# Third product of a block row moved into the next row, partial sums taken up in another order

## The chip, the cores and the metric

The kernel runs on one NeuronCore of a Trainium2 chip. The metric is device time of one execution in microseconds (us). A core has five engines that run side by side, each with its own instruction queue in program order: TensorE (PE, matmuls; PEld is its weight load), VectorE (DVE), ScalarE (ACT), GpSimd (POOL) and SyncE (SP, which here only issues DMAs). They wait for each other through semaphores. TensorE writes its results to PSUM, eight banks, and the other engines bring them to SBUF.

## The reference

Attention with two softmaxes that factor, then a two-layer network over all tokens:

```python
q_s = exp(q - max_d q) / sum_d        # over the head dimension
k_s = exp(k - max_s k) / sum_s        # over the sequence
kv  = einsum('bhsd,bhse->bhde', k_s, v)
x   = einsum('bhsd,bhde->bhse', q_s, kv)   # as 4608 tokens x 512
h   = x @ w_in                             # 512 x 2048
out = maximum(0.01 * h, h) @ w_out         # 2048 x 512
```

q, k and v are 8 batches x 8 heads x 576 x 64, in float32.

## The kernel before, in words

The 4608 tokens are nine tiles of 512. Attention of later batches runs between the matmuls of earlier tiles. For tiles 1 to 6 a plain scheme holds: layer 1 (`layer1`, L561) gives sixteen blocks of 128 hidden features, `leaky` (L571) on ScalarE makes the activations `g`, and layer 2 (`layer2_at`, L938) takes sixteen bf16 matmuls for each 128 tokens (a "tsub"), each ended by a ScalarE copy and a store.

Tiles 7 (called A, `TA`) and 8 (B8, `TB`) are done together, by a scheme that computes a 2x2 block product with seven block products instead of eight, at the cost of sums. Two stages matter.

The first is layer 1 of both tiles: eight block rows, `pair_layer1(i)` (L1027). The token sums s1 to s4 are made once by VectorE (`token_sums`, L831), the weight sums t1 to t4 of each row by GpSimd, two rows ahead (`in_weight_sums`, L811), with `b22`, a float32r copy of a weight block that has two buffers. The products of a row, each two matmuls of 128x512 (bf16 for the first two, float32r for the others), are: the first product `pair_first(i)` into bank px, issued a row ahead and copied out as e1 by ScalarE; t2·s2 added into px, copied out as u2 by VectorE; the second product into bank pw, to which e1 is added; t3·s3 into px, copied out as u3 by VectorE; t1·s1 into bank py, to which u3 is added; t4·a22 into px; and the third product b22·s4, added into py, to which u2 is added. A product that adds into a bank must wait until the copy out of that bank is done. ScalarE's `leaky` turns the sums into activations.

Between the products stand "fills" (`between(n)`, L1067): single layer 2 matmuls of tile 6, whose tsubs 1 to 3 were kept back for that (48 fills; tsub 0 is done ahead of row 0). The order on every engine is the order in which this Python code issues instructions; no planner changes it. The adds of u2 and their `leaky` are put off into the next row by the list `held`.

The second stage is layer 2 of both tiles, L1191 to L1222, again seven products for each tile: first, second, sixth, fifth, seventh, fourth, third (each sixteen matmuls of 128x256). First to second are bf16, the others float32r on row sums r1, r2, r3, r4 made by VectorE (`sums`, `row_sums`), and c22, a copy by ScalarE. r1 and r3 of tile 7 are made ahead in four blocks (`sums_ahead`), three by GpSimd, the last by VectorE. After first, sixth and seventh ScalarE takes a snapshot of the accumulating bank (`snap`: e1, u2, u3), and the next product into that bank must wait for it. `c11`, `c12` and `c22` are VectorE adds that finish quarters of the output. `put` (L1121) issues their DMAs; for tile 8 every other one is issued from ScalarE's queue:

```python
A = dict(t=TA, ..., issue=(nc.sync, nc.sync))
B8 = dict(t=TB, ..., issue=(nc.sync, nc.scalar))
```

Of the kernel before, what the change touches and what calls it, by code (L numbers as in the profile page):

```python
# [26 lines left out]
def kernel(  # L27
# [9 lines left out]
    nc = tc.nc  # L37
# [533 lines left out]
    def leaky(o, ph):  # L571
        nc.scalar.activation(out=o, in_=ph, func=AF.Prelu, alpha=LEAKY_SLOPE)  # L572
# [365 lines left out]
    def layer2_at(t, g, tsub, pool=psO_pool, tag="pout"):  # L938
        po = pool.tile([P, O], FP32, name="pout", tag=tag)
        for j in range(NF):  # L940
            layer2(po, g, tsub, j)
            if j == NF - 1:
                store(t * TT + tsub * P, po, nc.scalar.copy)
            if j % 4 == 3:
                run(t, 16 + 4 * tsub + j // 4)
            yield

    for t in range(1, TA):
        g_sb = []
        for j in range(NF):  # L950
            ph = psB_pool.tile([P, TT], FP32, name="ph", tag=BANK_TAG)
            layer1(j, ph, t * TT, TT)
            if j % 2 == 0:
                g_sb.append(g_pool.tile([P, 2, TT], BF16, name="gj"))
            leaky(g_sb[j // 2][:, j % 2], ph)
            run(t, j)
        for tsub in range(NTS if t < TA - 1 else 1):
            for _ in layer2_at(t, g_sb, tsub, *((psB_pool, BANK_TAG) if t == TA - 1 else ())):
                pass


# [4 lines left out]
    def g7_rows(i):  # L966
        if i == 0:
            g7_pairs.extend(g_pool.tile([P, 2, TT], BF16, name="gj") for _ in range(2))
        for fh in range(2):
            if i < 2:  # L970
                g7[fh * NH + i] = g7_pairs[fh][:, i]
            elif i < 6:
                g7[fh * NH + i] = spent(4 * (4 + fh) + i - 2)
            else:
                g7[fh * NH + i] = spent(4 * 6 + 2 * fh + i - 6)
# [19 lines left out]
    def late_rows(name, n, pool):  # L995
        late[name] = pool.tile([P, NH, M2], F32R, name=n)

    def sums_ahead(n):
        if n == 0:
            for name in ("r3", "r1"):  # L1000
                late_rows(name, name, late["ahead"])
        (ms, h0), (_, h1) = g7_blocks(0)[n], g7_blocks(1)[n]
        for name, x, y, op in (("r1", h1(0), h1(1), ALU.add), ("r3", h0(0), h1(0), ALU.subtract)):
            eng = nc.vector if n == 3 else nc.gpsimd
            eng.tensor_tensor(out=late[name][:, ms], in0=x, in1=y, op=op)

    def bank():
        return psB_pool.tile([P, TT], FP32, name="pp", tag=BANK_TAG)

    def product(ps, w, a, first=True):  # L1010
        for c in range(2):
            nc.tensor.matmul(ps, lhsT=w(c), rhs=a(c), start=(first and c == 0), stop=(c == 1), skip_group_check=True)  # L1012

    def add(o, ps, e):
        nc.vector.tensor_tensor(out=o, in0=ps, in1=e, op=ALU.add)  # L1015

    of = lambda n: (lambda c: late[n][:, c])
    keep = lambda n: late["pool"].tile([P, TT], FP32, name=n)
    firsts, held = {}, []

    def pair_first(i):
        ps, e1 = bank(), keep("e1")
        product(ps, lambda c: w_in_sb[:, c, i * P : (i + 1) * P], lambda c: xT[:, c, XA])
        nc.scalar.copy(out=e1, in_=ps)
        firsts[i] = ps, e1

    def pair_layer1(i, fills):  # L1027
        px, e1 = firsts[i]
        u2, u3 = keep("u2"), keep("u3")
        g7_rows(i)  # L1030
        product(px, of(("t2", i)), of("s2"), False)
        for fn in held:
            fn()
        nc.vector.tensor_copy(out=u2, in_=px)  # L1034
        pw = bank()
        product(pw, lambda c: w_in_sb[:, 2 + c, i * P : (i + 1) * P], lambda c: xT[:, 2 + c, XA])
        if i + 1 < NH:
            pair_first(i + 1)
        add(e1, pw, e1)
        leaky(g7[i], e1)  # L1040
        between(fills[0])
        product(px, of(("t3", i)), of("s3"), False)
        nc.vector.tensor_copy(out=u3, in_=px)
        py = bank()
        product(py, of(("t1", i)), of("s1"))
        between(fills[1])
        add(u3, py, u3)
        leaky(g8(NH + i), u3)
        if i == 0:
            nc.gpsimd.tensor_copy(out=gate, in_=u3[:, 0:1])  # L1050
        product(px, of(("t4", i)), of("a22"), False)
        leaky(g8(i), px)
        between(fills[2])
        product(py, of(("b22", i)), of("s4"), False)
        held[:] = [lambda: add(u2, py, u2), lambda: leaky(g7[NH + i], u2)]
        if i + 2 < NH:
            in_weight_sums(i + 2)
        if i in (2, 4, 6):
            sums_ahead(i // 2 - 1)
# [7 lines left out]
    def between(n):  # L1067
        for _ in range(n):
            next(fill)

    pair_first(0)
    between(2)
    for i in range(NH):
        pair_layer1(i, (2, 2, 2) if i else (1, 2, 1))
    for fn in held:
        fn()
    next(fill, None)
    sums_ahead(3)
    pairs.close()
    last_pool = ctx.enter_context(tc.tile_pool(name="late3", bufs=1, reuse_waits="tile"))  # L1080

# [6 lines left out]
    def product2(ps, a, w, each=False, turns=False, first=True):  # L1088
        order = [(i, m) for i in range(2) for m in range(NH)]
        if turns:  # L1090
            order = [(i, m) for m in range(NH) for i in range(2)]
        for i, m in order:
            nc.tensor.matmul(  # L1093
                ps[i],
                lhsT=a(m)[:, i * P : (i + 1) * P],
                rhs=w(m),
                start=(first and m == 0 and (each or i == 0)),
                stop=(m == NH - 1 and (each or i == 1)),
                skip_group_check=True,
            )  # L1100

    def row_sums(wide, name, n, pool, op, x, y, eng=nc.vector):
        late_rows(name, n, pool)
        for (ms, h0), (_, h1) in zip(wide(0), wide(1)):
            view = lambda s: late[s][:, ms].bitcast(FP32) if isinstance(s, str) else (h0, h1)[s[0]](s[1])
            o = late[name][:, ms]
            if op is None:
                nc.scalar.copy(out=o, in_=view(x))
            else:
                eng.tensor_tensor(out=o, in0=view(x), in1=view(y), op=op)  # L1110
# [3 lines left out]
    plain_w = lambda fh: (lambda m: w_out_sb[:, fh * NH + m, E1])  # L1114
    gu = lambda: g_pool.tile([P, 2, H2], FP32, name="gu", tag="gj")
    out_pairs = lambda: [osb_pool.tile([P, O], FP32, name="out_sb") for _ in range(2)]
    last_pairs = lambda n: [last_pool.tile([P, O], FP32, name=f"{n}{i}") for i in range(2)]
    A = dict(t=TA, g=lambda n: g7[n], wide=g7_wide, each=False, issue=(nc.sync, nc.sync))
    B8 = dict(t=TB, g=g8, wide=g8_wide, each=True, issue=(nc.sync, nc.scalar))

    def put(z, o, half, i, cols):  # L1121
        for n, issue in enumerate(z["issue"]):
# [11 lines left out]
    def first(z):  # L1134
        if z["each"]:
            z["x"] = banks2(True)
        else:
            z["xx"] = psB_pool.tile([P, 2, H2], FP32, name="pq", tag=BANK_TAG)
            z["x"] = [z["xx"][:, i] for i in range(2)]
        product2(z["x"], plain_g(z["g"], 0), plain_w(0), z["each"], turns=True)  # L1140
        snap(z, "e1")

    def second(z):
        z["w"] = banks2(False, psO_pool, "pout")
        product2(z["w"], plain_g(z["g"], 1), plain_w(1), turns=True)

    def sixth(z):
        product2(z["x"], rows("r2"), rows("v2"), z["each"], first=False)
        snap(z, "u2")

    def fifth(z):
        z["y"] = banks2(z["each"])
        product2(z["y"], rows("r1"), rows("v1"), z["each"])

    def seventh(z):
        product2(z["x"], rows("r3"), rows("v3"), z["each"], first=False)
# [11 lines left out]
    def c11(z):  # L1168
        for i in range(2):
            add(z["o1"][i][:, E1], z["w"][i], z["e1"][:, i])  # L1170
            put(z, z["o1"][i], 0, i, E1)
# [9 lines left out]

    def sums(z, n):
        pool = late["ahead"] if n == "r3" else last_pool
        row_sums(z["wide"], n, n, pool, *dict(
            r2=(ALU.subtract, "r1", (0, 0)),
            r3=(ALU.subtract, (0, 0), (1, 0)),
            r4=(ALU.subtract, (0, 1), "r2"),
            c22=(None, (1, 1), None),
        )[n])

    A["o1"], B8["o1"] = out_pairs(), last_pairs("o1")  # L1191
    first(A)
    sums(A, "r2")
    first(B8)
    sums(A, "r4")
    sums(A, "c22")
    second(A)
    c11(A)
    second(B8)
    sixth(A)  # L1200
    fifth(A)
    late["r1"] = strip("r1").rearrange("p a b -> p (a b)")[:, 0 : NH * M2].rearrange("p (m t) -> p m t", t=M2)
    for (ms, _), (_, h1) in zip(g8_wide(0), g8_wide(1)):
        nc.vector.tensor_tensor(out=late["r1"][:, ms], in0=h1(0), in1=h1(1), op=ALU.add)  # L1204
    c11(B8)
    sums(B8, "r2")
    seventh(A)
    A["o2"], B8["o2"] = out_pairs(), last_pairs("o2")
    sixth(B8)
    c22(A)  # L1210
    fourth(A)
# [42 lines left out]
```

## Time and profile before

| | |
|---|---|
| median of 3 runs | 282.3 us (282.01 to 282.64) |
| the profiled execution's own time | 282.73 us |
| its span, first to last instruction | 280.9 us |
| mean granted TensorE clock | 0.997 |
| TensorE busy | 273.1 us (97%) |
| VectorE busy | 216.8 us (77%) |
| ScalarE busy | 170.2 us (61%) |
| GpSimd busy | 81.2 us (29%) |

A line of the timeline has the start (us from the span's start), the duration, the engine, the source line, the operation, the tiles (out<-in) and shapes, and how many like it were merged (x4); in brackets how long the engine was idle just before, and what released it. Lines of a window view have the window, its length, each engine's busy time in it (with the number of instructions) in the order PE, PEld, DVE, ACT, POOL, then the granted TensorE clock, the DMA engines' busy share and GB/s. Ends of matmuls are modelled, so the distance from start to start is the firmer figure.

### The profile page before, as it was taken

What the parts mean: (1) busy time and instruction counts of PE and PEld (TensorE: products, weight loads), DVE (VectorE), ACT (ScalarE), POOL (GpSimd) and SP (SyncE); (2) the same over time, 40 slices, a digit from 0 to 9 for tenths busy, and PEclk for the clock granted to TensorE, in tenths of its full rate; (3) what the DMA queues carried; (4) which work ended last, traced back from release to release, by engine and by line L of the source; (5) the groups of instructions that cost most, each with busy time, mean ns of one, the idle gap of its engine ahead of it and who ended that gap; (6) DMA issues with size and microseconds to landing.
All of it is one profiled execution on the core that took longest, in us unless ns stands there. A gap on an engine that the chain in (4) does not pass through costs nothing. (4 is left out here: it accounts for less than half of the span.)

```text
span 280.9 us, 5223 instructions
## 1 busy us (share of the span) xinstructions
PE 273.1 (97%) x2018; PEld 147.7 (53%) x2018; DVE 216.8 (77%) x303; ACT 170.2 (61%) x302; POOL 81.2 (29%) x103
## 2 busy tenths in 40 slices
PE   8899999999999999999999999999999999999994
PEld 3378644444444444444444444454444555569994
DVE  2995995899999939957794698949958767679951
ACT  3976663783498457754675458664664666654241
POOL 2867360159003004000400084002011798800000
PEclk9999999999999999999999999999999999999998
DMA  7999999987996797099309930430701010101254
GB/s 235 331 209 322 240 256 271 394 277 217 258 389 213 102 386 255 2 228 398 116 4 267 384 84 2 84 77 0 160 0 40 0 37 0 40 19 31 65 113 113
DMA packets 40488, 46.48 MB, mean 165 GB/s; under 512 B 18832, under 2 KB 24208, under 8 KB 40464
## 3 DMA queue, kind: packets, MB, share of 16 engines
q1 hardware_dynamic: 36480, 41.43, 49.5%
q0 software_dynamic: 3504, 4.20, 8.6%
q10 hardware_dynamic: 480, 0.52, 0.6%
q8 instruction: 16, 0.26, 0.4%
q14 instruction: 8, 0.07, 0.1%
HBM read 36.70 MB, written 9.44 MB: 164 GB/s over the span
## 5 line engine op out<-in xcount | busy, mean ns | idle before, releaser
L584 PE MATMUL pout<-w_out_sb,gj 128*128 128x512 bf16 x448 | 103.7, 380 | 0.0
L563 PE MATMUL ph<-xT,w_in_sb 128*128 128x512 bf16 (+1 forms) x512 | 98.8, 352 | 0.3 <-DMA w_in_sb<-in_moe_w_in_dram 0.3
L572 ACT ACTIVATE gj<-ph 128x512 bf16<-128x512 f32 x112 | 63.5, 602 | 19.0 <-PE ph L563 18.5
L563 PEld LDWEIGHTS <-w_in_sb 128*128 128x128 bf16 x512 | 49.7, 98 | 47.6 <-DMA w_in_sb<-in_moe_w_in_dram 0.6
L584 PEld LDWEIGHTS <-gj 128*128 128x128 bf16 x448 | 41.8, 98 | 51.8 <-issue 4.6
L218 POOL CAST vb<-v_raw 128x1152 bf16<-128x1152 f32 x13 | 19.8, 1551 | 83.7 <-DMA v_raw<-in_v_dram 66.4
L578 ACT COPY out_sb<-pout 128x512 f32<-128x512 f32 x24 | 14.0, 584 | 34.8 <-PE pout L584 18.0
L321 DVE TENSOR_REDUCE qsum<-qe 128x36 f32<-128x2304 bf16 (+5 forms) x13 | 20.1, 1542 | 6.4 <-ACT qe L312 6.2
L206 ACT ACTIVATE ke<-k_raw 128x2304 bf16<-128x2304 f32 (+2 forms) x13 | 18.0, 1384 | 8.1 <-DVE k_raw L198 7.6
L328 DVE TENSOR_TENSOR qe<-qe,qrec 128x2304 bf16<-128x2304 bf16 (+5 forms) x13 | 21.5, 1656 | 0.4
L245 DVE TENSOR_REDUCE qmax<-q_raw 128x36 f32<-128x2304 f32 (+5 forms) x13 | 20.0, 1540 | 0.5 <-DMA q_raw<-in_q_dram 0.5
L312 ACT ACTIVATE qe<-q_raw 128x2304 bf16<-128x2304 f32 (+5 forms) x13 | 17.2, 1321 | 4.1 <-POOL q_raw L304 3.1
L198 DVE TENSOR_TENSOR k_raw<-k_raw,kall 128x1152 f32<-128x1152 f32 (+2 forms) x10 | 18.1, 1822 | 0.3
L304 POOL TENSOR_TENSOR q_raw<-q_raw,qmax 128x512 f32<-128x512 f32 (+3 forms) x7 | 11.8, 1680 | 21.2 <-DVE qmax L245 20.9
L1015 DVE TENSOR_TENSOR u<-pp,u 128x512 f32<-128x512 f32 x16 | 11.1, 692 | 8.6 <-PE pp L1012 7.8
L1012 PE MATMUL pp<-s,t 128*128 128x512 f32 x48 | 14.9, 419 | 0.8 <-issue 0.3
L572 ACT ACTIVATE xT<-u 128x512 bf16<-128x512 f32 x14 | 8.8, 630 | 10.9 <-DVE u L1015 10.8
L160 DVE TENSOR_TENSOR t<-t 128x256 f32<-128x256 f32 (+2 forms) x22 | 14.3, 652 | 0.7
L500 ACT CAST xT<-po 128x448 bf16<-128x448 f32 (+3 forms) x31 | 13.3, 513 | 1.6 <-PE po L479 1.6
L361 DVE RECIPROCAL krec<-pokv 128x2 f32<-128x2 f32 x8 | 1.3, 165 | 16.7 <-PE pokv L479 16.7
L304 DVE TENSOR_TENSOR q_raw<-q_raw,qmax 128x2304 f32<-128x2304 f32 (+1 forms) x6 | 13.2, 2202 | 0.2
L790 POOL TENSOR_TENSOR t<-w_in_sb 128x256 fp32r<-128x256 bf16 x16 | 11.4, 711 | 3.3 <-PE pp L1012 3.3
(125 smaller groups left out, 326.0 us busy)
## 6 DMA issues: line engine op xcount, KB each, us to landing
out_dram<-out_sb SPq DMA_DIRECT2D x60, 128.0 KB, 3.9
q_raw<-in_q_dram SPq DMA_DIRECT2D x6, 1152.0 KB, 9.1
v_raw<-in_v_dram SPq DMA_DIRECT2D x6, 1152.0 KB, 11.7
k_raw<-in_k_dram SPq DMA_DIRECT2D x5, 1152.0 KB, 6.3
k_raw<-in_k_dram SPq DMA_DIRECT2D x6, 576.0 KB, 6.5
v_raw<-in_v_dram SPq DMA_DIRECT2D x4, 576.0 KB, 8.0
w_in_sb<-in_moe_w_in_dram POOLq DMA_DIRECT2D x7, 256.0 KB, 6.9
w_out_sb<-in_moe_w_out_dram POOLq DMA_DIRECT2D x6, 256.0 KB, 9.4
```

The source lines that it names most:

```text
L198: eng.tensor_tensor(out=ks, in0=ks, in1=st[b]["kall"][:, hs].unsqueeze(2).to_broadcast([P, n, R, D]), op=ALU.subtract,)
L206: nc.scalar.activation(out=st[b]["ke"][:, :, hs].rearrange("p r h d -> p h r d"), in_=st[b]["k"][:, hs], func=AF.Exp,)
L218: eng.tensor_copy(out=o, in_=i)
L245: nc.vector.tensor_reduce(out=o, in_=st[b]["q"][:, hs, rs], axis=AX.X, op=ALU.max)
L304: eng.tensor_tensor(out=qs, in0=qs, in1=st[b]["qmax", rs.start, hs.start].unsqueeze(3).to_broadcast([P, m, n, D]), op=ALU.subtract,)
L312: nc.scalar.activation(out=q_cols(b, rs, hs).rearrange("p r h d -> p h r d"), in_=st[b]["q"][:, hs, rs], func=AF.Exp,)
L321: nc.vector.reduce_sum(out=qsum, in_=q_cols(b, rs, hs), axis=AX.X)
L328: nc.vector.tensor_tensor(out=qes if out is None else out, in0=qes, in1=st[b]["qrec", rs.start, hs.start].unsqueeze(3).to_broadcast([P, n, ...
L563: nc.tensor.matmul(ph, lhsT=w_in_sb[:, cb, j * P : (j + 1) * P], rhs=xT[:, cb, c0 : c0 + n], start=(cb == 0 and first), stop=(cb == NB - 1 ...
L572: nc.scalar.activation(out=o, in_=ph, func=AF.Prelu, alpha=LEAKY_SLOPE)
L584: nc.tensor.matmul(pout, lhsT=g_sb[j // 2][:, j % 2, tsub * P : (tsub + 1) * P], rhs=w_out_sb[:, j, os], start=(j == 0), stop=(j == NF - 1),)
L1012: nc.tensor.matmul(ps, lhsT=w(c), rhs=a(c), start=(first and c == 0), stop=(c == 1), skip_group_check=True)
```

## The change

Five parts.

1. Tile 6's tsub 0 is done after the function that follows it in the text, and row 0's first product is issued after ten of its sixteen fills. Its copy e1 thus stands ahead of the store's copy on ScalarE.
2. In row 0 the second product, with its add and its `leaky`, is issued ahead of t2·s2, and u2 is copied by ScalarE.
3. In the other rows VectorE's copy u2 comes first, then the second product and the third product of the row before, each with its add; the list `held` is gone. The fills are spread anew: (0, 3, 3) in most rows instead of (2, 2, 2).
4. In the second layer VectorE's sums have another order: r1's last block, r2 of tile 7, r1 of tile 8, then `c11(A)`, r3's last block, r2 of tile 8, `c11(B8)`, and r4 of tile 7 after them. r1 and r2 of tile 8 have names and buffers of their own.
5. `c11(B8)` is issued ahead of `sixth(A)` instead of behind `fifth(A)`. Tile 8's first output pair lies in two buffers of the activation pool.

The number of matmuls of each kind is the same.

```diff
-        for tsub in range(NTS if t < TA - 1 else 1):
-            for _ in layer2_at(t, g_sb, tsub, *((psB_pool, BANK_TAG) if t == TA - 1 else ())):
+        for tsub in range(NTS if t < TA - 1 else 0):
+            for _ in layer2_at(t, g_sb, tsub):
                 pass
...
-    def sums_ahead(n):
+    def sums_ahead(n, names=("r1", "r3")):
...
+    def pair_second(i):
+        e1 = firsts[i][1]
+        ps = bank()
+        product(ps, lambda c: w_in_sb[:, 2 + c, i * P : (i + 1) * P], lambda c: xT[:, 2 + c, XA])
+        add(e1, ps, e1)
+        leaky(g7[i], e1)
+
+    def pair_third(i):
+        py, u2 = thirds[i]
+        product(py, of(("b22", i)), of("s4"), False)
+        add(u2, py, u2)
+        leaky(g7[NH + i], u2)
+
     def pair_layer1(i, fills):
-        px, e1 = firsts[i]
+        px = firsts[i][0]
         u2, u3 = keep("u2"), keep("u3")
         g7_rows(i)
+        if i == 0:
+            pair_second(i)
+            between(1)
         product(px, of(("t2", i)), of("s2"), False)
-        for fn in held:
-            fn()
-        nc.vector.tensor_copy(out=u2, in_=px)
-        pw = bank()
-        product(pw, lambda c: w_in_sb[:, 2 + c, i * P : (i + 1) * P], lambda c: xT[:, 2 + c, XA])
+        if i:
+            nc.vector.tensor_copy(out=u2, in_=px)
+            pair_second(i)
+            pair_third(i - 1)
+        else:
+            nc.scalar.copy(out=u2, in_=px)
         if i + 1 < NH:
             pair_first(i + 1)
-        add(e1, pw, e1)
-        leaky(g7[i], e1)
         between(fills[0])
...
         between(fills[2])
-        product(py, of(("b22", i)), of("s4"), False)
-        held[:] = [lambda: add(u2, py, u2), lambda: leaky(g7[NH + i], u2)]
...
-    pair_first(0)
-    between(2)
+    for n, _ in enumerate(layer2_at(TA - 1, g_sb, 0, psB_pool, BANK_TAG)):
+        if n == 9:
+            pair_first(0)
     for i in range(NH):
-        pair_layer1(i, (2, 2, 2) if i else (1, 2, 1))
-    for fn in held:
-        fn()
+        pair_layer1(i, ((2, 3, 2), *[(0, 3, 3)] * 5, (0, 3, 2), (1, 3, 1))[i])
+    pair_third(NH - 1)
     next(fill, None)
-    sums_ahead(3)
...
-    last_pairs = lambda n: [last_pool.tile([P, O], FP32, name=f"{n}{i}") for i in range(2)]
+    last_pairs = lambda: [gu().rearrange("p a b -> p (a b)") for _ in range(2)]
...
+    def r1_last():
+        late["r1b"] = strip("r1b").rearrange("p a b -> p (a b)")[:, 0 : NH * M2].rearrange("p (m t) -> p m t", t=M2)
+        for (ms, _), (_, h1) in zip(g8_wide(0), g8_wide(1)):
+            nc.vector.tensor_tensor(out=late["r1b"][:, ms], in0=h1(0), in1=h1(1), op=ALU.add)
...
-    A["o1"], B8["o1"] = out_pairs(), last_pairs("o1")
+    A["o1"], B8["o1"] = out_pairs(), last_pairs()
     first(A)
+    sums_ahead(3, ("r1",))
     sums(A, "r2")
     first(B8)
-    sums(A, "r4")
+    r1_last()
     sums(A, "c22")
     second(A)
     c11(A)
+    sums_ahead(3, ("r3",))
     second(B8)
+    sums(B8, "r2")
+    c11(B8)
     sixth(A)
+    sums(A, "r4")
     fifth(A)
-    late["r1"] = strip("r1").rearrange("p a b -> p (a b)")[:, 0 : NH * M2].rearrange("p (m t) -> p m t", t=M2)
-    for (ms, _), (_, h1) in zip(g8_wide(0), g8_wide(1)):
-        nc.vector.tensor_tensor(out=late["r1"][:, ms], in0=h1(0), in1=h1(1), op=ALU.add)
-    c11(B8)
-    sums(B8, "r2")
     seventh(A)
```

More of the change, by code (lines that the diff above doesn't have):

```diff
@@ L1002, in sums_ahead @@
         (ms, h0), (_, h1) = g7_blocks(0)[n], g7_blocks(1)[n]
-        for name, x, y, op in (("r1", h1(0), h1(1), ALU.add), ("r3", h0(0), h1(0), ALU.subtract)):
+        ops = dict(r1=(h1(0), h1(1), ALU.add), r3=(h0(0), h1(0), ALU.subtract))
+        for name in names:
+            x, y, op = ops[name]
             eng = nc.vector if n == 3 else nc.gpsimd
@@ L1018 @@
     keep = lambda n: late["pool"].tile([P, TT], FP32, name=n)
-    firsts, held = {}, []
+    firsts, thirds = {}, {}
     def pair_first(i):
@@ L1045, in pair_layer1 @@
         product(py, of(("t1", i)), of("s1"))
+        thirds[i] = py, u2
         between(fills[1])
@@ L1116 @@
     out_pairs = lambda: [osb_pool.tile([P, O], FP32, name="out_sb") for _ in range(2)]
-    last_pairs = lambda n: [last_pool.tile([P, O], FP32, name=f"{n}{i}") for i in range(2)]
-    A = dict(t=TA, g=lambda n: g7[n], wide=g7_wide, each=False, issue=(nc.sync, nc.sync))
-    B8 = dict(t=TB, g=g8, wide=g8_wide, each=True, issue=(nc.sync, nc.scalar))
+    last_pairs = lambda: [gu().rearrange("p a b -> p (a b)") for _ in range(2)]
+    A = dict(t=TA, g=lambda n: g7[n], wide=g7_wide, each=False, issue=(nc.sync, nc.sync), r1="r1", r2="r2")
+    B8 = dict(t=TB, g=g8, wide=g8_wide, each=True, issue=(nc.sync, nc.scalar), r1="r1b", r2="r2b")
     def put(z, o, half, i, cols):
@@ L1147, in sixth @@
     def sixth(z):
-        product2(z["x"], rows("r2"), rows("v2"), z["each"], first=False)
+        product2(z["x"], rows(z["r2"]), rows("v2"), z["each"], first=False)
         snap(z, "u2")
@@ L1152, in fifth @@
         z["y"] = banks2(z["each"])
-        product2(z["y"], rows("r1"), rows("v1"), z["each"])
+        product2(z["y"], rows(z["r1"]), rows("v1"), z["each"])
     def seventh(z):
@@ L1183, in sums @@
         pool = late["ahead"] if n == "r3" else last_pool
-        row_sums(z["wide"], n, n, pool, *dict(
-            r2=(ALU.subtract, "r1", (0, 0)),
+        name = "r2b" if z is B8 and n == "r2" else n
+        row_sums(z["wide"], name, name, pool, *dict(
+            r2=(ALU.subtract, z["r1"], (0, 0)),
             r3=(ALU.subtract, (0, 0), (1, 0)),
-            r4=(ALU.subtract, (0, 1), "r2"),
+            r4=(ALU.subtract, (0, 1), z["r2"]),
             c22=(None, (1, 1), None),
         )[n])
-    A["o1"], B8["o1"] = out_pairs(), last_pairs("o1")
+    def r1_last():
[3 more added lines that the diff above has]
+    A["o1"], B8["o1"] = out_pairs(), last_pairs()
     first(A)
+    sums_ahead(3, ("r1",))
     sums(A, "r2")
     first(B8)
-    sums(A, "r4")
+    r1_last()
     sums(A, "c22")
@@ L1198 @@
     c11(A)
+    sums_ahead(3, ("r3",))
     second(B8)
+    sums(B8, "r2")
+    c11(B8)
     sixth(A)
+    sums(A, "r4")
     fifth(A)
-    late["r1"] = strip("r1").rearrange("p a b -> p (a b)")[:, 0 : NH * M2].rearrange("p (m t) -> p m t", t=M2)
-    for (ms, _), (_, h1) in zip(g8_wide(0), g8_wide(1)):
-        nc.vector.tensor_tensor(out=late["r1"][:, ms], in0=h1(0), in1=h1(1), op=ALU.add)
-    c11(B8)
-    sums(B8, "r2")
     seventh(A)
-    A["o2"], B8["o2"] = out_pairs(), last_pairs("o2")
+    A["o2"], B8["o2"] = out_pairs(), [last_pool.tile([P, O], FP32, name=f"o{i}") for i in range(2)]
     sixth(B8)
```

## The prediction

> **What bounds the kernel now.** I read the page first (which engine fills the span), then busy time by stretch from 207.29 us on (no instruction ahead of it moves), then the timeline, all engines.
>
> ```profile
> span 280.9 us, 5223 instructions
> ...
> PE 273.1 (97%) x2018; PEld 147.7 (53%) x2018; DVE 216.8 (77%) x303; ACT 170.2 (61%) x302; POOL 81.2 (29%) x103
> ```
>
> ```profile
> 207.29:217.60 10.31, 9.68 (x49) 4.43 (x41) 8.90 (x12) 5.68 (x11) 1.75 (x5) 1.00 0.12 27
> 217.60:246.00 28.40, 28.37 (x122) 15.18 (x121) 19.65 (x31) 18.45 (x32) 23.50 (x35) 1.00 0.09 19
> 246.00:250.19 4.19, 4.06 (x18) 1.89 (x17) 2.99 (x5) 2.04 (x4) 0.00 (x0) 1.00 0.01 2
> 250.19:276.90 26.71, 26.61 (x225) 25.49 (x224) 19.78 (x28) 10.62 (x21) 0.00 (x0) 1.00 0.31 71
> ```
>
> TensorE is the bound, at full clock (the 1.00 behind the POOL column). The change moves matmuls and removes none, so only TensorE's waits can be won or lost. Modelled ends hide short waits in "busy", so I price by distances between starts.
>
> First block row 0. The columns are start, duration, engine, line.
>
> ```profile
> 207.29 3.63 PE L584 MATMUL pout<-w_out_sb,gj 128*128 128x512 bf16 x16
> ...
> 210.76 0.59 PE L1012 MATMUL pp<-xT,w_in_sb 128*128 128x512 bf16 x2
> ...
> 211.44 0.59 ACT L1024 COPY e<-pp 128x512 f32<-128x512 f32 x1
> ...
> 212.13 0.70 PE L1012 MATMUL pp<-s,t 128*128 128x512 f32 x2 [0.35 <-issue]
> 212.25 1.22 DVE L790 TENSOR_TENSOR s<-xT,s 128x1024 fp32r<-128x1024 bf16 x1
> ...
> 213.39 0.68 DVE L1034 COPY u<-pp 128x512 f32<-128x512 f32 x1
> ...
> 213.99 0.68 DVE L1015 TENSOR_TENSOR e<-pp,e 128x512 f32<-128x512 f32 x1
> ...
> 214.22 1.17 PE L1012 MATMUL pp<-s,t 128*128 128x512 f32 x4 [0.29 <-DVE u L1034]
> ...
> 214.70 0.63 ACT L572 ACTIVATE gj<-e 128x512 bf16<-128x512 f32 x1 [0.37 <-DVE e L1015]
> ...
> 215.23 0.60 PE L584 MATMUL pout<-w_out_sb,gj 128*128 128x512 bf16 x2
> ```
>
> Two waits: t2·s2 for ScalarE's copy e1 (ends 212.03), and t3·s3 at 214.22 for VectorE's copy u2, which stood behind the token sum s4 (ends 213.47).
>
> A steady row (3), with the first line from row 1:
>
> ```profile
> 217.60 1.04 PE L1012 MATMUL pp<-xT,w_in_sb 128*128 128x512 bf16 x4
> ...
> 226.78 0.69 DVE L1015 TENSOR_TENSOR u<-pp,u 128x512 f32<-128x512 f32 x1 [1.00 <-PE pp L1012]
> 227.06 1.04 PE L1012 MATMUL pp<-xT,w_in_sb 128*128 128x512 bf16 x4
> ...
> 227.39 0.68 DVE L1034 COPY u<-pp 128x512 f32<-128x512 f32 x1
> ...
> 229.03 0.69 DVE L1043 COPY u<-pp 128x512 f32<-128x512 f32 x1 [0.36 <-PE pp L1012]
> 229.31 0.60 PE L584 MATMUL pout<-w_out_sb,gj 128*128 128x512 bf16 x2
> ...
> 229.87 0.70 PE L1012 MATMUL pp<-a,t 128*128 128x512 f32 x2
> ...
> 230.41 0.61 PE L584 MATMUL pout<-w_out_sb,gj 128*128 128x512 bf16 x2
> ...
> 231.79 1.04 PE L1012 MATMUL pp<-xT,w_in_sb 128*128 128x512 bf16 x4
> ```
>
> Each line with x4 here begins with a row's second product: 217.60 in row 1, 227.06 in row 3, and 231.79 a row (4.73) later. A bf16 matmul takes b = 0.217 (207.29 to 210.76 is sixteen). From 227.06 to 229.31 lie six of them and two float32r products (pairs of matmuls): a pair is p = (2.25 − 1.30) / 2 = 0.475. A row is 10b + 5p = 4.545; the missing 0.19 is t4·a22, which should come at 229.31 + 2b = 229.74 but waits for the copy u3 (229.03 + 0.69 = 229.72) until 229.87, and then needs 0.54 instead of p. So VectorE to TensorE takes 0.15, and TensorE to VectorE 0.19 (t3·s3 ends at 229.31 − p = 228.84).
>
> The second layer of tiles 7 and 8:
>
> ```profile
> 250.19 0.61 PE L1093 MATMUL pq<-w_out_sb,gj 128*128 128x256 bf16 x4
> ...
> 251.77 1.29 DVE L1005 TENSOR_TENSOR r<-xT 128x512 fp32r<-128x512 bf16 x2 [0.70 <-ACT xT L572]
> ...
> 252.98 0.69 DVE L1110 TENSOR_TENSOR r<-r,gj 128x512 fp32r<-128x512 f32 x1
> ...
> 255.32 0.69 DVE L1110 TENSOR_TENSOR r<-gj,r 128x512 fp32r<-128x512 bf16 x1
> ...
> 257.11 8.26 PE L1093 MATMUL pq<-v,r 128*128 128x256 f32 x64
> 257.66 0.75 DVE L1015 TENSOR_TENSOR out_sb<-pq,gu 128x256 f32<-128x256 f32 x2
> ...
> 258.32 2.35 DVE L1204 TENSOR_TENSOR r<-xT 128x1024 fp32r<-128x1024 bf16 x2
> 259.30 0.59 ACT L1132 COPY gu<-pq 128x512 f32<-128x512 f32 x1 [2.89 <-PE pq L1093]
> 260.59 0.76 DVE L1015 TENSOR_TENSOR o<-pq,gu 128x256 f32<-128x256 f32 x2
> ...
> 261.05 1.38 ACTq L1124 DMA_DIRECT2D out_dram<-o  x2
> 261.25 2.36 DVE L1110 TENSOR_TENSOR r<-r,xT 128x1024 fp32r<-128x1024 f32 x2
> 263.14 0.59 ACT L1132 COPY gu<-pq 128x512 f32<-128x512 f32 x1 [3.25 <-DMA out_dram<-o]
> ...
> 265.20 2.08 PE L1093 MATMUL pq<-v,c 128*128 128x256 f32 x16
> 267.12 2.08 PE L1093 MATMUL pq<-o,r 128*128 128x256 f32 x16
> ```
>
> A float32r product takes 1.92 (265.20 to 267.12). The four from 257.11 to 265.20 should take 7.75 (the first, after a bf16 one, 1.99: its snapshot starts at 259.30, some 0.2 behind its end) and take 8.09: 0.34 is sixth(B8)'s wait for r2 of tile 8, ready at 263.61.
>
> **The change, part by part.** Call T the start of first(A), 250.19 now.
>
> Row 0. e1's copy moves ahead of the store's copy on ScalarE, and the first product goes after ten of tile 6's fills, so t2·s2 finds all it needs. But u2's copy goes to ScalarE, whose order becomes: leaky of e1, then that copy. The leaky needs VectorE's add of e1, which comes where u2's copy stands now, behind s4: 213.39 to 214.07. Leaky from 214.10 to 214.73 (0.03 and 0.63, as at 214.70), copy until about 215.24, and TensorE 0.1 later (212.03 to 212.13) at 215.34. By then it has done 25 bf16 matmuls and one product from 207.29, in both kernels, so t3·s3 is 1.12 later. From there 1.01 for the two products (214.22 to 215.23), 3b, p, 2b and p bring the start of row 1's second product to 218.39, against 217.60.
>
> Rows 1 to 6. The third product b22·s4 now comes in the next row, behind the second product. From a row's t2·s2 the gap to t3·s3 is 4b + p = 1.34, while u2's copy takes 0.19 + 0.68 + 0.15 = 1.02: hidden. VectorE then has copy u2, add e1, add u2 of the row before, and copy u3 at 0.61 spacing (226.78 to 227.39): 0.19 + 3 × 0.61 = 2.02, about when t3·s3 lets it start (1.34 + p + 0.19 = 2.00). It is ready at 2.02 + 0.69 + 0.15 = 2.86; t4·a22 now has three fills ahead and comes at 1.34 + 2p + 3b = 2.94. Hidden by 0.08; with that cover gone a row gets its 0.19 back. An unstalled pair between fills stands nowhere in the trace: p (t3·s3 follows fills so) or 0.54 bound it; I take p, the same product behind the same kind of fill. Five rows of 4.545 and row 6 with one fill less (4.33): 241.11, then 245.44.
>
> The b22 buffer comes free a product later, so GpSimd's weight sums may wait a little in its queue; it is busy 23.50 of 28.40 there and each sum is wanted two rows on: nothing. SP's DMAs keep their order. Tile 8's o1 takes two activation buffers of tile 6, whose last reader is a fill ahead of T: nothing.
>
> Row 7. No first product stands between, so u3's copy (2.86) is later than t4·a22 could start (2.73): 2.86 + 0.54 + b + p = 4.09. T = 249.53: 0.66 won.
>
> Second layer. VectorE now does r1's last block, r2(A), r1 of tile 8, c11(A), r3's block, r2 of tile 8, c11(B8), and only then r4(A). r2 of tile 8 is early, so the 0.34 goes. But c11(B8)'s adds are late: VectorE's chain starts at T + 1.58 (251.77) and takes 0.60 (half of 251.77 to 252.98) + 2.34 (252.98 to 255.32) + 2.27 (258.32 to 260.59) + 0.66 (257.66 to 258.32) + 0.60 + 2.27 = 8.74, with no wait for TensorE in it: the first add at T + 10.32. The two output DMAs of c11(B8) that ScalarE issues stand, in its order, now ahead of both of tile 7's snapshots. Queued behind them is the snapshot u2, which frees the bank for seventh(A). The issues begin 0.46 behind the add (260.59 to 261.05), last 1.38, then 0.59 of copy and 0.1: T + 12.85. TensorE could start seventh(A) at T + 6.92 + 1.99 + 1.92 = T + 10.83. So 2.02 is lost, and some 0.07 in the first pair behind it.
>
> How far the issues hold the copy is not shown before: 0 to 1.38. I take 1.38, since the two issues themselves follow one another in ScalarE's row. [...]
>
> The sum against the profiled execution's 282.73 (its median stands 0.43 lower): −0.66 (T) − 0.34 + 2.02 + 0.07 = +1.09, so 283.8 there and 283.4 for the median 282.3. The tail behind TensorE's end keeps its shape.
>
> **The rivals.** 0.2% (0.56 us) is about what the measurement tells from no change.
>
> No change: the copy waits for the adds but not for the issues. It could start at T + 10.32 + 0.76 + 0.04, and seventh(A) at T + 11.81: 0.98 lost, −0.66 − 0.34 + 0.98 + 0.07 = +0.05: 282.4. For it: an issue isn't counted as engine work. Against: the order on the queue.
>
> Faster: the issue of a DMA doesn't hold ScalarE at all, wait included, so snapshot u2 runs at T + 9.1 and seventh(A) is on time: −0.66 − 0.34 = −1.0: 281.3. It decides once the copy is done by T + 10.83. For it: no ScalarE copy of the old kernel stands late because of an issue. Against: none could be late, as the next copy (263.14) came 0.7 behind the issues' end and waited for seventh(A).
>
> Slower still: the 0.08 of cover in the rows is gone, or an unstalled pair costs 0.54. Rows 1 to 6 then keep 4.73, six times 0.19 = 1.1: 284.5. For it: VectorE's four steps fit to 0.02. Against: its spacings have held to 0.01.
>
> **How the numbers follow.** Forecast 0.56, no change 0.14, faster 0.16, slower still 0.14. The forecast's own range is 282.9 to 284.0 (the issues at 0.5 each, or a row's wait half back). The 8-in-10 range takes in no change, half of each of the outer cases: 281.4 to 284.4. Slower takes 0.14 and all but 0.05 of the forecast: 0.65; same 0.17; faster 0.18.
>
> **What would show it.** Right: t3·s3 of row 0 near 215.3, behind ScalarE's copy; rows 4.55 apart without a wait at t4·a22; first(A) near 249.5; a gap of 2 us at the start of seventh(A), ended by ScalarE's gu copy, itself behind two issues on its queue; no wait at sixth(B8). Wrong: first(A) later than 250.2, or seventh(A) right behind fifth(A).

## The result and the profile after

The changed kernel takes 285.05 us (median of six runs, 283.50 to 285.34) against 282.25 for the kernel before: the ratio of the means is 1.0087, 95% interval 1.0061 to 1.0113. Slower, as forecast, but by 2.8 us where 1.1 was said, and outside the range of 281.4 to 284.4. The six runs fall into two groups. Four take 285.01 to 285.34 with a mean granted TensorE clock of 0.993 or 0.994; two take 283.50 and 284.03, with 0.999 and 1.000. The profiled execution (285.34) is one of the four.

The page of the changed kernel, and its busy time by stretch. The columns are the window, its length, then PE, PEld, DVE, ACT, POOL with instructions, the granted clock, DMA share, GB/s:

```profile
span 283.5 us, 5218 instructions
...
PE 272.3 (96%) x2018; PEld 148.3 (52%) x2018; DVE 215.4 (76%) x302; ACT 170.1 (60%) x303; POOL 81.4 (29%) x103
...
PEclk9999999999999999999999999999997999999999
```

```profile
200.00:216.00 16.00, 14.03 (x78) 6.47 (x77) 11.06 (x11) 9.80 (x18) 0.74 (x2) 1.00 0.17 37
216.00:219.50 3.50, 3.50 (x10) 1.71 (x9) 1.04 (x2) 1.23 (x2) 2.21 (x5) 0.51 0.00 0
219.50:258.00 38.50, 38.50 (x202) 23.24 (x201) 28.38 (x43) 24.43 (x44) 22.54 (x33) 1.00 0.10 21
258.00:260.40 2.40, 2.40 (x22) 2.40 (x21) 2.40 (x5) 0.00 (x0) 0.00 (x0) 1.00 0.16 36
260.40:263.90 3.50, 1.62 (x15) 1.42 (x13) 3.50 (x6) 0.59 (x1) 0.00 (x0) 1.00 0.49 110
```

PE is "busy" for all of 216.00 to 219.50, but with ten matmuls, and the granted clock there is 0.51: the 7 in the row of digits. The trace's record of the clock puts the half clock from 216.04 to 219.46, 3.4 us. In the last window PE is busy 1.62 of 3.50 at full clock: a wait. What stands ahead of the slow stretch ("issue" in brackets means that the profile shows nothing that released the engine; ACTq is a DMA issue on ScalarE's queue):

```profile
206.90 2.33 PE L584 MATMUL pout<-w_out_sb,gj 128*128 128x512 bf16 x10
...
211.91 0.60 PE L1014 MATMUL pp<-xT,w_in_sb 128*128 128x512 bf16 x2
212.35 0.59 PE L584 MATMUL pout<-w_out_sb,gj 128*128 128x512 bf16 x2
212.99 0.69 DVE L1017 TENSOR_TENSOR e<-pp,e 128x512 f32<-128x512 f32 x1
213.72 0.63 ACT L572 ACTIVATE gj<-e 128x512 bf16<-128x512 f32 x1 [2.13 <-DVE e L1017]
214.25 0.57 ACT L1055 COPY u<-pp 128x512 f32<-128x512 f32 x1
...
214.92 1.16 PE L1014 MATMUL pp<-s,t 128*128 128x512 f32 x4 [1.97 <-issue]
...
215.92 1.39 PE L584 MATMUL pout<-w_out_sb,gj 128*128 128x512 bf16 x3
...
216.75 1.42 PE L1014 MATMUL pp<-a,t 128*128 128x512 f32 x2
...
219.59 0.60 PE L1014 MATMUL pp<-xT,w_in_sb 128*128 128x512 bf16 x2
```

The chain of row 0 is the forecast one (VectorE's add, leaky, ScalarE's copy, t3·s3). TensorE stands idle for 1.97 us, does t3·s3 and t1·s1 at full rate, and then runs at half.

The second layer:

```profile
251.02 0.61 PE L1108 MATMUL pq<-w_out_sb,gj 128*128 128x256 bf16 x4
...
261.36 0.76 DVE L1017 TENSOR_TENSOR gu<-pq,gu 128x256 f32<-128x256 f32 x2
...
261.81 1.40 ACTq L1139 DMA_DIRECT2D out_dram<-gu  x2
...
263.25 0.59 ACT L1147 COPY gu<-pq 128x512 f32<-128x512 f32 x1 [6.00 <-issue]
263.88 2.17 PE L1108 MATMUL pq<-v,r 128*128 128x256 f32 x16 [1.88 <-ACT gu L1147]
...
277.42 2.08 PE L1108 MATMUL pq<-o,r 128*128 128x256 f32 x16
```

The snapshot starts 0.04 behind the end of the two issues (263.21), 1.13 behind the second add (262.12), though sixth(A) was long done; seventh(A) follows it.

Where the time went, measured from tile 6's first fill of that stage (206.90 after, 207.29 before, as the front part came out 0.39 shorter in this execution): first(A) comes after 44.12 instead of 42.90 (+1.22), the last product's start another 26.40 behind it instead of 24.61 (+1.79). Together +3.01, less 0.39: the span is 2.6 longer.

### The profile page after: what moved, and what is told of

Same layout as the page of the kernel before. It is cut to its first block, busy times and chain, and to the rows that moved or that the text cites. A ratio compares the mean times of both kernels' runs of the same rounds, so it can differ in the third digit from the quotient of the medians.

```text
span 283.5 us, 5218 instructions
## 1 busy us (share of the span) xinstructions
PE 272.3 (96%) x2018; PEld 148.3 (52%) x2018; DVE 215.4 (76%) x302; ACT 170.1 (60%) x303; POOL 81.4 (29%) x103
## 4 chain that ended last, share of the span: by engine, by line
PE 90%; DVE 5%; DMA 2%; issue 1%; ACT 0%; ACTq 0%; SPq 0%; DVEq 0%
PE pout L584 35%; PE ph L563 34%; PE pp L1014 10%; PE pq L1108 7%; DMA k_raw<-in_k_dram 2%; PE po L479 2%; DVE t L160 1%; PE pokv L341 1%; DVE r2b L1125 1%; PE pkv L341 1%; DVE r1b L1210 1%; PE pkv L419 0%; DVE k_raw L410 0%; DVE gu L1017 0%; ACTq L1139 0%
## 5 line engine op out<-in xcount | busy, mean ns | idle before, releaser
L1014 PE MATMUL pp<-s,t 128*128 128x512 f32 x48 | 17.0, 463 | 2.0 <-issue 2.0
L1051 DVE COPY u<-pp 128x512 f32<-128x512 f32 x7 | 4.8, 692 | 10.2 <-PE pp L1014 8.9
L160 DVE TENSOR_TENSOR t<-k_raw 128x512 f32<-128x512 f32 (+1 forms) x11 | 11.2, 1016 | 1.3 <-DMA k_raw<-in_k_dram 1.2
```

The costliest lines, as they stand in the source:

```text
L160: nc.vector.tensor_tensor(out=o, in0=i0, in1=i1, op=ALU.max)
```

## The experiments

Two theories of the clock had to be told apart. A: row 0's wait also costs the clock. B: the drop of the clock has another cause. A third, C, is about the other wait: seventh(A) waits for VectorE's sums, not for the snapshot behind the issues. Nothing is left out of any kernel below; they are compared with the kernel before at 281.89 us (first four) and, on another chip, 281.97 (last four).

**Row 0's copy first.**

```diff
+        if not late_leaky:          # in pair_second; True in row 0
             leaky(g7[i], e1)
...
             nc.scalar.copy(out=u2, in_=px)
+            leaky(g7[i], firsts[i][1])
```

> The changed kernel, with one thing moved: in row 0 ScalarE copies u2 ahead of the leaky of e1, so the copy no longer stands behind VectorE's add of e1. Nothing is left out. Theory A: TensorE's wait of 1.97 us at t3 s3 of row 0 goes, and with it the stretch of 3.4 us at half the granted clock that follows it (another 1.7 us); the mean granted clock is 0.999 to 1.000 in every run, and the time is 285.05 - 2.0 - 1.7 = about 281.4 us, the same within 0.5 us in all runs. Rival B: the drop of the granted clock has another cause and stays: 285.05 - 2.0 = about 283.0 us, with 0.993 to 0.994 in most runs. In both the wait of about 2 us at seventh(A) stays.

Twelve runs: six of 281.22 to 281.55 at 0.999 to 1.000, six of 282.63 to 282.90 at 0.993 or 0.994. Neither theory as it was put: row 0's wait is gone and its slow stretch too, but the profiled execution (282.90) has one elsewhere, behind the other wait:

```profile
216.00:219.50 3.50, 3.50 (x17) 1.97 (x16) 3.09 (x5) 2.00 (x5) 3.32 (x6) 1.00 0.00 0
219.50:258.00 38.50, 38.50 (x216) 24.89 (x214) 29.05 (x44) 22.45 (x41) 20.43 (x30) 1.00 0.13 28
258.00:260.40 2.40, 0.52 (x5) 0.40 (x4) 2.40 (x4) 0.58 (x1) 0.00 (x0) 1.00 0.48 109
260.40:263.90 3.50, 3.50 (x20) 3.50 (x20) 0.18 (x2) 0.59 (x1) 0.00 (x0) 0.54 0.00 0
```

Here seventh(A)'s wait of 1.88 us (258.1 to 260.0) is followed by half clock. So the drop follows either wait, and not in every run.

**The snapshot first.**

```diff
-    c11(B8)
     sixth(A)
+    c11(B8)
```

> The changed kernel, with one thing moved: c11(B8) is issued behind sixth(A), so that on ScalarE the snapshot u2 of tile 7 stands ahead of the two output DMAs; VectorE's, TensorE's and SP's orders are the same. Nothing is left out. Theory A (the two DMA issues, waiting for VectorE's late adds, hold the snapshot): seventh(A) starts 1.9 to 2.1 us earlier, directly behind fifth(A): about 283.1 us in runs with a granted clock of 0.993 to 0.994, about 281.6 us in runs with 0.999 to 1.000. Rival C (seventh(A) waits for VectorE's late row sums, not for the snapshot): no change, 285 us. The wait in row 0 and the drop of the clock stay as they are, in about two runs of three.

Twelve runs: eight of 281.03 to 281.51 at 0.997 to 1.000, four of 282.66 to 283.21 at 0.992 or 0.993: a drop in one run of three, where two of three were expected. The three products sixth(A), fifth(A) and seventh(A), and ScalarE's rows, in the profiled execution, one of the eight:

```profile
255.94 5.99 PE L1108 MATMUL pq<-v,r 128*128 128x256 f32 x48
...
258.13 0.59 ACT L1147 COPY gu<-pq 128x512 f32<-128x512 f32 x1 [2.88 <-PE pq L1108]
259.81 1.39 ACTq L1139 DMA_DIRECT2D out_dram<-gu  x2
261.97 0.59 ACT L1147 COPY gu<-pq 128x512 f32<-128x512 f32 x1 [3.25 <-DMA out_dram<-gu]
```

The issues take the same 1.39, now with nothing waiting behind them, and TensorE no longer waits at seventh(A): its 48 matmuls stand in one row of 5.99. VectorE's and TensorE's orders are untouched, so C falls. Row 0's wait of 1.96 is there, without a drop in this execution; from the first fill first(A) takes 42.46 here and 44.12 in the changed kernel's profile. The drop costs 1.66 there. The medians of the two groups of runs lie 1.5 apart in the first experiment, 1.6 in this one and 1.4 in the changed kernel.

**Both.**

> The changed kernel with both moves: ScalarE copies u2 of row 0 ahead of the leaky of e1, and the snapshot of tile 7 stands ahead of the two output DMAs. Nothing is left out. Theory A: both waits and the slow clock go: 285.05 - 2.0 - 1.7 - 2.0 = about 279.3 us, granted clock 0.999 to 1.000 in every run, faster than the kernel before by about 1.0%. Rivals: 281 us if the clock drop stays (B), 281.4 us if seventh(A) still waits (C), more if the time won in one place turns into a wait at the next.

279.15 (278.97 to 279.20), 0.997 to 1.000 in all four runs; a ratio of the means of 0.9901 (0.9888 to 0.9913): this version beats both kernels. With neither wait no run of the four has a drop.

```profile
215.50:219.00 3.50, 3.50 (x17) 2.04 (x17) 3.20 (x5) 2.01 (x4) 3.24 (x7) 1.00 0.00 0
260.40:263.90 3.50, 3.50 (x31) 3.50 (x31) 3.02 (x4) 0.99 (x3) 0.00 (x0) 1.00 0.00 0
```

**A shorter wait.** With the snapshot first, VectorE copies u2 in row 0, ahead of its add.

```diff
-            nc.scalar.copy(out=u2, in_=px)
+            nc.vector.tensor_copy(out=u2, in_=px)
+            second_sums(i, pw)        # row 0's add and leaky of e1
```

> As the kernel with both moves, but in row 0 VectorE copies u2, behind its token sums and ahead of its add of e1, as it did in the kernel before: TensorE waits about 0.9 us at t3 s3 instead of 1.97 us or none. Nothing is left out. Theory A1 (a wait of TensorE costs the clock only when it is long; shorter waits cost themselves): clock 0.999 to 1.000 in every run, 279.3 + 0.9 = about 280.2 us. A2 (any wait of this size costs the clock too): about 0.994 in some runs, and these take about 281.9 us.

280.01 (279.92 to 280.14), 0.997 or 0.998 in all five. The wait is 0.87 and costs 0.86 over the version with both moves: itself and nothing else.

That left open why 1.9 us drops the clock in some runs only. Theory W: what counts is how long TensorE was idle within one stretch of some 3.4 us, the length of the changed kernel's slow one (216.04 to 219.46), and above a threshold the clock drops. Theory H: a wait of any length drops it by chance, in about half of the runs. The next three stretch row 0's wait by making the same copy of u2 several times, with the snapshot first throughout.

```diff
+            for _ in range(2):        # 5 in the longest; for 1.5 us, VectorE's copy twice
                 nc.scalar.copy(out=u2, in_=px)
```

> As the kernel in which VectorE copies u2 of row 0, but VectorE makes that copy twice, so that TensorE waits 0.87 + 0.6 = about 1.5 us at t3 s3. Nothing is left out. About 280.6 us. Theory W: no run with a drop of the clock (0.997 to 1.000 throughout), since 1.5 us is below the threshold. Theory H: about a third to a half of the runs at 0.992 to 0.994 and about 282.2 us.

> As the kernel with the snapshot ahead of the DMAs (row 0's wait left in), but ScalarE makes row 0's copy u2 twice, so that TensorE waits 1.96 + 0.55 = about 2.5 us at t3 s3. Nothing is left out. The wait alone costs 0.55: about 281.8 us in runs with a granted clock of 0.997 to 1.000, about 283.4 us in runs with a drop (0.992 to 0.994). Theory W (the clock is set by how much of a free-running stretch of some 3.4 us TensorE was idle; with 14 drops in the 30 runs that had a wait of 1.9 to 2.0 us this puts the threshold near 1.9 us): drops in about 6 of 10 runs. Theory H (a wait of any length drops the clock by chance, in about half of the runs): 5 of 10, the same as before.

> As the kernel with the snapshot ahead of the DMAs, but ScalarE makes row 0's copy u2 five times, so that TensorE waits 1.96 + 4 x 0.55 = about 4.2 us at t3 s3. Nothing is left out. Theory W: every run has the drop, since 4.2 us covers more than 1.9 us of some 3.4 us stretch wherever that stretch begins: 281.2 + 2.2 + 1.7 = about 285.1 us, granted clock 0.99 or below in all, and all runs close together. Theory H: half of the runs without a drop, at about 283.4 us.

t3·s3 of row 0 in the profiles of the 0.87, 1.5, 2.5 and 4 us kernels; the wait stands in the brackets:

```profile
213.54 1.16 PE L1014 MATMUL pp<-s,t 128*128 128x512 f32 x4 [0.87 <-DVE u L1061]
214.23 1.17 PE L1014 MATMUL pp<-s,t 128*128 128x512 f32 x4 [1.60 <-DVE u L1062]
215.34 2.04 PE L1014 MATMUL pp<-s,t 128*128 128x512 f32 x4 [2.57 <-issue]
217.15 1.75 PE L1014 MATMUL pp<-s,t 128*128 128x512 f32 x4 [4.44 <-issue]
```

Measured waits and clocks (a run with a mean clock of 0.994 or less is counted as a drop; the kernel before was never under 0.996 in the 34 runs beside these, and the 0.997 of its profile comes from the clock's fall at 279.43, behind the last matmul, where it costs nothing):

| TensorE's wait, us | runs with a drop | times, us |
|---|---|---|
| none (both moves) | 0 of 4 | 278.97 to 279.20 |
| 0.87 | 0 of 5 | 279.92 to 280.14 |
| 1.60 | 0 of 7 | 280.98 to 281.31 |
| 1.88 to 1.97 (changed kernel, first two experiments) | 14 of 30 | two groups each |
| 2.57 | 5 of 5 | 283.15 to 283.61 |
| 4.44 | 4 of 4 | 285.30 to 286.26 |

Theory H (any wait, half of the runs) falls at both ends: none in 7, then 9 in 9. Theory W's order is right, with 5 of 5 where it said 6 in 10. The changed kernel has two such waits in a run, the others one. The 1.60 kernel is 0.5 slower than I expected at full clock, of which the longer wait explains 0.1 and row 7 another 0.2 (there t4·a22 comes 0.99 behind its three fills, 246.59 to 247.58, instead of 0.78 in the 0.87 kernel); the rest is open. Two of the 4.44 kernel's runs read 0.987 and are 0.8 longer than the others, as if two stretches had been slow; no trace of these two was kept. The slow stretch of its profiled execution:

```profile
212.00:217.10 5.10, 0.71 (x4) 0.10 (x1) 1.44 (x2) 3.50 (x7) 0.00 (x0) 1.00 0.24 51
217.10:217.50 0.40, 0.35 (x2) 0.34 (x3) 0.00 (x0) 0.40 (x1) 0.00 (x0) 0.97 0.00 0
217.50:220.90 3.40, 3.40 (x10) 1.62 (x9) 1.38 (x2) 0.67 (x2) 1.13 (x3) 0.50 0.00 0
220.90:222.00 1.10, 1.10 (x6) 0.59 (x6) 0.01 (x1) 0.60 (x1) 1.10 (x3) 1.00 0.00 0
```

Again 3.4 us at 0.50. It begins 0.33 behind the end of the wait; in the changed kernel it was 1.1, behind seventh(A) in the first experiment 0.7, and in the 2.57 kernel it begins at 215.06, 0.28 ahead of the end of the wait. Its start is thus not tied to the wait, but its length is the same each time. That fits a clock decided at the ends of fixed stretches of 3.4 us: a stretch with enough idle time in it gives a slow one next. A wait of 1.9 us then drops the clock only where nearly all of it falls into one stretch.

The traces bear this out. Each of the four slow stretches amid matmuls is recorded with a length of 3.413 us, and in each of the ten traces all changes of the clock lie whole multiples of that apart: in the changed kernel's, the clock falls at 216.04 and again, behind the span's end, at 284.31, which is 20 x 3.413 later. The first recorded change comes 4.15 to 7.19 us behind the span's start, elsewhere in each run (4.42 in the changed kernel's, 6.37 in that of before), so the stretches do not begin with the kernel. Cut along them, these are the stretches with the waits of the changed kernel (the first two), the first and the second experiment:

```profile
212.63:216.04 3.41, 1.44 (x7) 0.79 (x6) 1.44 (x3) 1.59 (x3) 0.00 (x0) 1.00 0.35 77
260.42:263.83 3.41, 1.59 (x14) 1.38 (x12) 3.41 (x6) 0.58 (x1) 0.00 (x0) 1.00 0.48 109
257.29:260.71 3.42, 1.54 (x13) 1.34 (x13) 3.27 (x6) 0.58 (x1) 0.00 (x0) 1.00 0.42 96
212.97:216.39 3.42, 1.81 (x8) 1.15 (x9) 1.34 (x3) 1.59 (x3) 0.00 (x0) 1.00 0.18 41
```

Length less PE's busy time is 1.97, 1.82, 1.88 and 1.61 us idle. The first and the third are followed by half clock, the second and the fourth are not: there the wait lies across the end of a stretch. Over all ten traces, from the first recorded change on, every stretch with 1.88 us idle or more is followed by a slow one and none with 1.82 or less (idle time by modelled ends of matmuls). A wait of 1.95 us must then have all but some 0.1 us in one stretch, which 3.41 - 1.95 + 0.2 = 1.66 of 3.41 us of possible starts allow: about half, an estimate that fits 14 of 30.

**The first stage alone.** Rows, fills and row 0 of the first experiment, with the second layer's order as before.

> The first stage of the changed kernel (rows, fills and row 0, with ScalarE's copy u2 ahead of the leaky of e1), with the second layer's sums and output order as in the kernel before. Nothing is left out. Both theories: no wait of TensorE in row 0 and none of 2 us at seventh(A), so a granted clock of 0.997 to 1.000 in every run. If the rows and row 0 carry the gain as worked out, 281.9 - 2.4 = about 279.5 us, with the wait of 0.34 us at sixth(B8) back; if the second layer's new order is worth more than that, above 279.7 us.

279.58 (279.37 to 279.64), 0.996 to 1.000, a ratio of the means of 0.9914 (0.9900 to 0.9927): 2.39 us faster than the kernel before. The version with both moves was 2.74 faster, so the second layer's order is worth 0.35 once the snapshot stands first. The traces show where: the four products from sixth(A) on take 8.11 here (254.06 to 262.17), with sixth(B8)'s wait, and 7.75 with both moves (253.78 to 261.53).

## Why the prediction was wrong

*Row 0's wait.* Right in mechanism and size: t3·s3 was put 8.05 behind the first fill and came at 8.02 (206.90 to 214.92).

*What follows it.* This step failed: "From there 1.01 for the two products (214.22 to 215.23), 3b, p, 2b and p bring the start of row 1's second product to 218.39". The two products did take about that, but the fills and pairs behind them were priced at the full-clock rates of a trace in which TensorE never waited longer than 0.35 us in this part. On the changed kernel's axis 218.39 is 218.00; it came at 219.59, 1.59 late. The wait of 1.97 costs once as a wait and, in most of the six runs, once more through the clock (1.66). So the term that was put at nothing, without a reason, is the clock behind a wait: the sum's -0.66 at first(A) became +1.22, of which the clock is 1.66 and the rest of the stage 0.22. No rival held this: each priced a wait at its own length. Without a drop the kernel takes 283.50 or 284.03, within the forecast's own range of 282.9 to 284.0 but for 0.03.

*Rows 1 to 6.* Right. What stands around t4·a22 in row 1, then two second products of later rows and t4·a22 in the row that the second of them begins:

```profile
221.88 0.82 PE L584 MATMUL pout<-w_out_sb,gj 128*128 128x512 bf16 x3
...
222.35 0.81 PE L1014 MATMUL pp<-a,t 128*128 128x512 f32 x2
...
223.00 0.82 PE L584 MATMUL pout<-w_out_sb,gj 128*128 128x512 bf16 x3
...
228.71 0.61 PE L1014 MATMUL pp<-xT,w_in_sb 128*128 128x512 bf16 x2
...
233.28 0.61 PE L1014 MATMUL pp<-xT,w_in_sb 128*128 128x512 bf16 x2
...
235.35 0.68 DVE L1060 COPY u<-pp 128x512 f32<-128x512 f32 x1
...
235.57 0.82 PE L584 MATMUL pout<-w_out_sb,gj 128*128 128x512 bf16 x3
...
236.18 0.70 PE L1014 MATMUL pp<-a,t 128*128 128x512 f32 x2
...
236.72 0.61 PE L584 MATMUL pout<-w_out_sb,gj 128*128 128x512 bf16 x2
```

A row is 4.57 (4.545 said, 4.73 before). In row 1 three fills and the pair take 1.12 (221.88 to 223.00), so the pair takes 0.47: the p of 0.475 was the right choice for a pair that needn't wait. In the later row they take 1.15: u3's copy ends at 236.03, and 0.15 later the product starts, so the cover of 0.08 is used up and exceeded by some 0.03. "Slower still" did not happen. In the second experiment's profile, which has no drop, first(A) came 42.46 behind the first fill, against 42.24 said; 0.14 of the difference is row 7 (4.23 instead of 4.09).

*Seventh(A).* Right: T + 12.86 measured (251.02 to 263.88), T + 12.85 said, and from T to the last product 1.79 was lost where the sum had 1.75 (-0.34 + 2.02 + 0.07). "No change" and "faster" both needed the copy to pass the issues, and the snapshot 0.04 behind their end refutes them. That the issues hold the copy for their whole 1.38 was the author's choice between 0 and 1.38, which no trace of the kernel before shows; here they took 1.40 (261.81 to 263.21), and all of it held the copy. sixth(B8) follows without a wait, as forecast. That the wait of 2 us there can cost the clock as well (the granted clock is 0.54 from 260.40 to 263.90 in the first experiment's profile) was missed in the same way; in the changed kernel's profiled execution it didn't, by little: 1.82 us of it fell into one stretch.

*The chances.* Slower had 0.65, and the direction held, by the mechanism that was named: the two runs without a drop (283.50 and 284.03) are slower than the kernel before as well. The size was wrong by one missing term.

## What to carry to other kernels

Where a change gives TensorE a wait, price it twice: its length, and what the matmuls behind it cost at half clock if the wait is near 2 us or longer (here a drop cost 1.4 to 1.7 us, and 1.88 us of idle time within one stretch of 3.41 were enough); a median over runs then mixes two groups, and the granted clock of each run tells which is which. Read each engine's queue around a moved instruction, DMA issues included: a copy that frees a bank belongs ahead of an issue that waits for another engine (the other order cost TensorE a wait of 1.88 us here). The change itself was good but for two positions in ScalarE's queue: with both mended it is 1.0% faster than the kernel before.

## What the runs showed of the hardware

- TensorE waits of 0.87 and 1.60 us brought no drop of the granted clock in 12 runs; 1.88 to 1.97 brought one in 14 of 30, 2.57 and 4.44 in nine of nine. A drop cost 1.4 to 1.7 us.
- In ten traces the granted clock changed only at whole multiples of 3.413 us from one another, at another place in each run: to one half behind stretches of that length with 1.88 us of TensorE's idle time or more, never behind those with 1.82 or less.
- Two DMA issues on ScalarE's queue, beside two on SP's, took 1.38 us in the kernel before, 1.40 in the changed one and 1.39 in the second experiment; in the changed kernel the copy queued behind them started 0.04 after their end (263.21, 263.25).
- A float32r pair between two groups of bf16 matmuls that needn't wait takes 0.47 (221.88 to 223.00 less three fills of 0.217), as the 0.475 taken.
